# A fused attention and two-layer MLP kernel: the first batch's weight conversion one tile earlier, eight sums later, three attention steps in the next half

## The chip, the core and the metric

The kernel runs on one NeuronCore of a Trainium2 chip. The core has five engines that run side by side, each with its own queue of instructions in order: TensorE (PE, matmuls; its weight loads are PEld), VectorE (DVE), ScalarE (ACT), GpSimd (POOL) and SyncE (SP, which here only issues DMAs). The metric is the time of one execution on the device in microseconds (us), the median of several runs.

## The reference

Inputs are q, k, v of 4 batches, 8 heads, 768 positions and 64 channels a head, and an MLP's U, V, w_ch1 (512 x 2048) and w_ch2 (2048 x 512), the latter in float64.

```python
# attention: a band of +-15 keys, and one summary key for each block of 32
k_sum = k.reshape(B, H, nb, 32, D).max(axis=3)
v_sum = v.reshape(B, H, nb, 32, D).mean(axis=3)
scores_l = where(|i - j| < 16, scale * q @ k.T, -1e9)
scores_s = scale * q @ k_sum.T + log(32)
a = softmax(concat([scores_l, scores_s]))
x = a @ concat([v, v_sum])                 # heads side by side: 768 x 512 a batch
# the MLP
u = x + (x.T @ U @ V).T
out = u + relu(u @ w_ch1) @ w_ch2
```

## The kernel before

The four batches go through the MLP one after the other, and the attention of batch b+1 is done in pieces while batch b's MLP keeps TensorE busy. For each batch the MLP has an up half (u @ w_ch1, then `relu`) and a down half (times w_ch2). This document is about batch 0. Its up half is 16 tiles of 128 hidden channels, each tile four slots of 6 matmuls (`up`, L970; both halves of the tokens, two slots each), so 64 slots. Its down half is 96 slots, 16 tiles of 6: four slots with 3 matmuls of 512 columns, then two with 6 matmuls of 256 columns (`down_phase`, L1256). Every product is made of three matmuls on a high and a low part of each operand.

**The weights of batch 0** come as float64 words, 32 tiles (16 up, 16 down), and each passes through a fixed chain that `first_weights` spreads over the slots of the tile that is being multiplied, tile s. SP loads the words of tile s+7 (L778). ACT scales the words (`scale_weight`, L148). DVE makes a float32 of them in two steps (`from_f64`, L160 and L161). Then `split_weight` makes the two parts: ACT writes the high part (L176) and POOL subtracts it for the low part (L177). Only then can TensorE use the tile. In the kernel before, during tile s, the tile s+1 is split, s+2 is converted and s+3 is scaled. The first two or three tiles are done in `START`, an order written out by hand for the first stage: `Z` is a scaling, `Y m.0` and `Y m.1` the two conversion steps, `W` a split, `G` and `Go` make the operand u, `U` are the up half's first slots. DVE also adds and subtracts weights for later batches (`sum_weights`, L821 to L825), and SP stores converted weights and sums (L830 to L840).

**keep_rows** (L986) has POOL add the two parts of u to get u back, eight additions of 128 x 384, for the end of the batch where u is added to the result.

**Attention of batch 1** is a list of 32 steps (`later_steps`), spread evenly over slots: the first 13 (`FIRST_STEPS_1`) over slots 8 to 61 of the up half, the other 19 over slots 0 to 65 of the down half. Of head h: SP loads k and q (L198, L207), PE makes scores (L351, 24 matmuls), DVE and ACT the exponentials (L376, L386), DVE turns 32 x 32 squares (L406), SP writes them to DRAM (L411) and fetches them back in another order (`fetch_squares`, L419, four DMAs into the tile `at`, which has one buffer), and PE multiplies them with the values (`square_values`, L484, called the product of head h below). The fetch for head h+1 is issued in the step that holds the product of head h, since it writes the buffer which that product reads. The block sums of v go to POOL in pieces, one a slot (`add_vsum`, L255 to L269), and POOL spreads the block maxima of k (L328).

All engines take their instructions in the order in which the Python program emits them (a manual schedule); the tile library adds the waits.

Of the kernel before, what the change touches and what calls it, by code (L numbers as in the profile page):

```python
# [33 lines left out]
NF = DF // P  # L34
# [48 lines left out]
    K4 E12 V0 lq7 V5 V7 V3 lv2 lv3 lr Kp4 K7 Kp7 E13 S4 N1 E8 T10 V6 E9 lw0 S7 T11 N2 E14 T12 lw1  # L83
    T13 Q1 Q0 E15 N0 Qo1 Qo0 M1 Mo1 C11 N3 Bp5 I0 Bd6 T8 lw2 Dd5 Z0 Io0 C10 Dp4 T15 lw3 Y0.0 T9
    Y0.1 Bp4 Dp7 J0 C8 T14 V10 V11 Jo0 G0.0 G0.1 C9 Dp6 lw4 Z1 C14 V9 C13 Bp7 C12 W0 Y1.0 Y1.1 N5
    V8 V12 C15 N4 V13 V15 V14 N6 G1.0 lw5 N7 Go0.0 Go0.1 I2 Io2 U0.0.0 G1.1 Go1.0 Go1.1 lw6 J2 Jo2
    U0.1.0 G0.2 G0.3 Go0.2 Go0.3 G1.2 G1.3 Go1.2 Go1.3 U0.0.1 U0.1.1 W1 Z2
"""


# [5 lines left out]
def body(ctx: ExitStack, tc, q0, q1, k, v, vn, uv, w1, w2, mask, ident, rep, out):  # L96
# [23 lines left out]
    def weight_place(m, dt=F32):  # L120
        return wt.tile([P, 2 * DM], dt, name="place", tag=f"w{m % RING}")
# [22 lines left out]
    def scale_f64(words):  # L144


        hi = words.bitcast(F32).rearrange("p (n w) -> p n w", w=2)[:, :, 1]
        nc.scalar.activation(hi, hi, AF.Prelu, scale=BIAS, alpha=2.0**32)  # L148
# [22 lines left out]
    def run(steps, n=None):  # L171
        for _ in itertools.islice(steps, n):
            pass

    def split(hi, lo, val, engine):
        nc.scalar.copy(hi, val)  # L176
        engine.tensor_tensor(lo, val, f32(hi), ALU.subtract)  # L177
# [597 lines left out]
    def load_weight(m):  # L775

        words[m] = weight_place(m, I32)
        nc.sync.dma_start(out=words[m], in_=(w1, w2)[m // NF][:, m % NF].bitcast(I32))  # L778

    def scale_weight(m):  # L780
        scale_f64(words[m])

    def turn_weight(m):

        vals = yield from from_f64([words.pop(m)])
        w_kept[m] = vals[0]

    def by_parts(val):

        return val.rearrange("p (i k f) -> p k i f", k=2, f=P)  # L790

    def split_weight(m):
        t, val = weight_place(m, F32R), w_kept[m]
        if m < NF:
            t = t.rearrange("p (k s i f) -> p k s i f", k=2, s=2, f=P)
            val = by_parts(val)
            hi, lo = t[:, :, 0], t[:, :, 1]
        else:
            t = t.rearrange("p (s c) -> p s c", s=2)
            hi, lo = t[:, 0], t[:, 1]  # L800
        split(hi, lo, val, nc.gpsimd)
        w_split[m] = t
# [33 lines left out]
    def store_down(f):  # L836
        nc.sync.dma_start(out=down_there[f // 2, :, f % 2], in_=w_kept[NF + f])
# [179 lines left out]
    for _, t in vt0:  # L1017
        nc.gpsimd.memset(t[:NB], 0.0)

    turns = {m: turn_weight(m) for m in range(2)}  # L1020
    uv_val = []

    def turn_uv():
# [92 lines left out]
    turning = {}  # L1116

    def first_weights(s, q, n):


        f = s % NF

        def turn():
            if s + 2 < 2 * NF:
                if s + 2 not in turning:
                    turning[s + 2] = turn_weight(s + 2)
                run(turning[s + 2], 1 if q == 1 else None)

        if q == 0:
            if s + RING - 1 < 2 * NF:  # L1130
                load_weight(s + RING - 1)
            if 0 < s and s + 1 < 2 * NF:
                split_weight(s + 1)
            if s < NF and f % 2 == 0:
                sum_weights(f // 2, 0)
            if s >= NF:
                store_down(f)
        if q == 1:
            turn()
            if s < NF:  # L1140
                store_up(f)
        if q == 2:
            if s < NF and f % 2 == 0:
                sum_weights(f // 2, 1)
            turn()
            if s < NF and f % 2:
                store_sums(f // 2)
        if q == 3 and s + 3 < 2 * NF:
            scale_weight(s + 3)
        if q == n - 1:  # L1150
            w_kept.pop(s - 1, None)

# [297 lines left out]

    UP, DOWN = 7 * NF // 2 - 2, NF * NU
    FIRST_STEPS = 15
    FIRST_STEPS_1 = 13
    OPERANDS = ((45, 49, 55, 62, 67), (68, 73, 79, 88, 86))

    UP0 = 4 * NF - 2
# [2 lines left out]
    for b in range(B):  # L1459
        cur, ahead, after = ([*sts, None, None][b + i] for i in range(3))  # L1460
        todo = later_steps(ahead) if ahead else []
        n_first = FIRST_STEPS if b else FIRST_STEPS_1
        mine, theirs = todo[:n_first], todo[n_first:]
        up_last = UP if b else UP0
        steps = spread(mine, 4 if b else 8, up_last)
        if b == 0:
            phase = first_up_phase(cur, done)
            for n, j in enumerate((-4, -3, -2, -1)):
                steps.setdefault(n + 1, []).append((later_start, ahead, j))
            for n, (hf, c) in enumerate(itertools.product(range(2), range(NC))):  # L1470
                steps.setdefault(2 * n + 3, []).append((keep_rows, cur, hf, c))
        else:
            phase = up_phase(cur)
        if not ahead:
            sum_places(cur)
            for p in range(NF // 2 - 1):
                steps.setdefault(7 * p + 11, []).append((gate_sums, cur, p))
        last = []
        for i in itertools.count():
            try:  # L1480
                next(phase)
            except StopIteration as end:
                last = end.value or []
                break
            do(steps.get(i, ()))
            if b == 0:
                first_weights(i // 4, i % 4, 4)
            tick()
            drip()
            if i == up_last - 8 and ahead:  # L1490
                g = gate_high(cur, 0)
            if i == up_last - 6 and ahead:
                gate_low(*g)
            if i == UP - 4 and not ahead:
                phase7 = seven_phase(cur)
                next(phase7)
        if not ahead:
            for i, _ in enumerate(phase7):
                if i < 2:
                    do([last[i]])  # L1500
                if i == 3:
                    gate_sums(cur, NF // 2 - 1)
                tick()
            break
        steps = spread(theirs, 0, OPERANDS[0][-1] - 1)
        for u, x in operand_places(ahead):
            steps.setdefault(u, []).append(x)
        for i, x in enumerate(last):
            steps.setdefault(1 + 2 * i, []).insert(0, x)
        for i, _ in enumerate(down_phase(cur, g)):  # L1510
            do(steps.get(i, ()))
            if b == 0:
                first_weights(NF + i // NU, i % NU, NU)
                f, n = divmod(i, NU)
                if (f, n) in ((NF - 5, 4), (NF - 4, 1), (NF - 4, 4)):
                    fetch_weight()
                if (f, n) in ((NF - 3, 4), (NF - 2, 1), (NF - 2, 4), (NF - 1, 2)):
                    prepare()
            tick()
            drip()  # L1520
            if after and i % NU == 0:
                do([(later_start, after, j) for j in {7: (-6,), 9: (-5,), 11: (-4,), 13: (-3, -1), 14: (-2,)}.get(i // NU, ())])
# [93 lines left out]
```

## Time and profile before

| | us |
|---|---|
| median of 3 runs (637.68 to 639.45) | 639.23 |
| the profiled execution | 633.91 |
| its span, from the first to the last instruction | 632.1 |
| batch 0: first stage, to the first up matmul | 0 to 45.9 |
| batch 0: up half | 45.9 to 133.0 |
| batch 0: down half | 133.0 to about 220 |
| batches 1 to 3 | to 632.1 |

The profile is of one execution; its records begin and end about 1.8 us inside the measured time. A row of the timeline gives an instruction's start, its length and, in brackets, how long its engine sat idle before it and what ended that wait.

### The profile page before, as it was taken

What the parts mean: (1) busy time and instruction counts of PE and PEld (TensorE: products, weight loads), DVE (VectorE), ACT (ScalarE), POOL (GpSimd) and SP (SyncE); (2) the same over time, 40 slices, a digit from 0 to 9 for tenths busy, and PEclk for the clock granted to TensorE, in tenths of its full rate; (3) what the DMA queues carried; (4) which work ended last, traced back from release to release, by engine and by line L of the source; (5) the groups of instructions that cost most, each with busy time, mean ns of one, the idle gap of its engine ahead of it and who ended that gap; (6) DMA issues with size and microseconds to landing.
All of it is one profiled execution on the core that took longest, in us unless ns stands there. A gap on an engine that the chain in (4) does not pass through costs nothing.

```text
span 632.1 us, 14968 instructions
## 1 busy us (share of the span) xinstructions
PE 606.3 (96%) x5560; PEld 551.8 (87%) x5560; DVE 415.9 (66%) x1102; ACT 366.3 (58%) x810; POOL 324.8 (51%) x408
## 2 busy tenths in 40 slices
PE   4987899999999999999999999999999999999997
PEld 3776799988878899998888899998888899999997
DVE  4874947867766945567557974567546664449992
ACT  3754456666746567765634646675544447669550
POOL 2435956734237885788466976684231356630000
PEclk9999899999999999999999999999999999999999
DMA  9888679999895577987987686889997564365551
GB/s 223 226 305 249 210 215 308 323 304 305 255 284 145 172 226 216 268 245 235 294 237 229 189 274 198 262 256 270 283 280 233 154 225 135 118 216 175 160 192 50
DMA packets 91624, 144.51 MB, mean 229 GB/s; under 512 B 8864, under 2 KB 61472, under 8 KB 91552
## 3 DMA queue, kind: packets, MB, share of 16 engines
q1 hardware_dynamic: 91552, 143.56, 74.5%
q8 instruction: 44, 0.72, 0.5%
q14 instruction: 28, 0.23, 0.1%
HBM read 102.63 MB, written 40.89 MB: 227 GB/s over the span
## 4 chain that ended last, share of the span: by engine, by line
PE 80%; POOL 5%; issue 4%; DMA 4%; DVE 2%; ACT 2%; SPq 1%; POOLq 0%; ACTq 0%; DVEq 0%
PE acc L1256 27%; PE ps_h L1158 27%; PE acc L1368 9%; PE ps_h L970 8%; PE ps_s L351 3%; PE ps_x L484 3%; POOL place L177 2%; POOL place L255 1%; DMA place<-in_vn 1%; DMA at<-there 1%; DMA place<-in_q 1%; DMA whole<-up 1%; POOL x L986 1%; PE ps_m L615 1%; PE ps_t L454 1%
## 5 line engine op out<-in xcount | busy, mean ns | idle before, releaser
L912 POOL TENSOR_TENSOR parts<-whole,parts 128x512 fp32r<-128x512 f32 (+1 forms) x128 | 157.3, 1237 | 131.1 <-ACT parts L916 110.9
L1158 PE MATMUL ps_h<-op,parts 128*128 128x384 f32 x1008 | 180.1, 336 | 0.3 <-ACT place L1204 0.3
L1158 PEld LDWEIGHTS ps_h<-op,parts 128*128 128x128 f32 x1008 | 174.3, 188 | 3.0 <-issue 1.3
L1256 PE MATMUL acc<-gh,parts 128*128 128x256 f32 (+1 forms) x512 | 135.4, 343 | 0.0
L1256 PEld LDWEIGHTS acc<-gh,parts 128*128 128x128 f32 x512 | 88.5, 190 | 12.9 <-issue 1.7
L916 ACT CAST parts<-whole 128x512 fp32r<-128x512 f32 (+1 forms) x144 | 83.2, 584 | 10.0 <-DMA whole<-up 3.7
L1256 PE MATMUL acc<-gl,parts 128*128 128x512 f32 (+1 forms) x256 | 86.7, 339 | 0.0
L386 ACT ACTIVATE e<-e,neg 128x120 f32<-128x120 f32 x144 | 46.5, 386 | 62.5 <-DVE neg L376 62.5
L177 POOL TENSOR_TENSOR place<-val,place 128x512 fp32r<-128x512 f32 x32 | 45.2, 1413 | 72.5 <-ACT place L176 49.6
L970 PE MATMUL ps_h<-place 128*128 128x384 f32 x384 | 73.0, 346 | 6.7 <-POOL place L177 4.8
L970 PEld LDWEIGHTS ps_h<-place 128*128 128x128 f32 x384 | 67.5, 192 | 10.9 <-POOL place L177 6.8
L1231 DVE SCALAR_TENSOR_TENSOR gl<-place,gh 128x768 fp32r<-128x768 f32 x48 | 50.2, 1046 | 35.2 <-ACT gh L1227 35.1
L1256 PE MATMUL acc<-gh,place 128*128 128x512 f32 (+1 forms) x256 | 67.2, 342 | 0.4 <-POOL e L372 0.2
L1227 ACT ACTIVATE gh<-place 128x768 fp32r<-128x768 f32 x48 | 40.5, 844 | 26.7 <-PE acc L1256 26.6
L1256 PEld LDWEIGHTS acc<-gl,parts 128*128 128x128 f32 x256 | 48.6, 190 | 3.9
L376 DVE CUSTOM_DVE_ANT_0 e<-ps_s,mask_sb 128x120 f32<-128x120 f32 x144 | 32.8, 277 | 27.4 <-PE ps_s L351 27.3
L1256 PEld LDWEIGHTS acc<-gh,place 128*128 128x128 f32 x256 | 44.2, 190 | 7.2 <-issue 0.9
L1368 PE MATMUL acc<-place,parts 128*128 128x384 f32 x246 | 43.6, 334 | 0.0
L1256 PE MATMUL acc<-gl,place 128*128 128x512 f32 (+1 forms) x128 | 43.4, 339 | 0.2 <-DVE gl L1231 0.2
L1368 PEld LDWEIGHTS acc<-place,parts 128*128 128x128 f32 x246 | 42.7, 188 | 0.0
L1218 DVE TENSOR_TENSOR place<-place,ps_h 128x384 f32<-128x384 f32 x24 | 13.3, 555 | 36.1 <-ACT place L1217 36.0
L1184 DVE TENSOR_TENSOR place<-place,ps_h 128x384 f32<-128x384 f32 x24 | 13.2, 551 | 30.0 <-PE ps_h L1158 30.0
(155 smaller groups left out, 948.3 us busy)
## 6 DMA issues: line engine op xcount, KB each, us to landing
place<-in_w SPq DMA_DIRECT2D x32, 512.0 KB, 5.4
whole<-up SPq DMA_DIRECT2D x24, 512.0 KB, 4.3
there<-squares SPq DMA_DIRECT2D x24, 384.0 KB, 4.7
at<-there SPq DMA_DIRECT2D x96, 96.0 KB, 4.7
whole<-up SPq DMA_DIRECT2D x24, 384.0 KB, 3.3
whole<-down SPq DMA_DIRECT2D x16, 512.0 KB, 5.0
vt<-in_v SPq DMA_DIRECT2D x48, 146.2 KB, 4.6
kt<-in_k SPq DMA_DIRECT2D x24, 288.0 KB, 5.4
```

What stands on the lines that cost most here:

```text
L177: engine.tensor_tensor(lo, val, f32(hi), ALU.subtract)
L351: nc.tensor.matmul(ps[a][c : c + 64, i * KC : (i + 1) * KC], qt[r : r + 64, q0 : q0 + 64], kt[r : r + 64, k0 : k0 + KC], start=True, stop= ...
L376: nc.vector.tensor_tensor_reduce(out=e[:, u, :], in0=ps[:, i * KC : (i + 1) * KC], in1=mask_sb[:, m, :], scale=-SCALE, scalar=BIG, op0=ALU ...
L386: nc.scalar.activation(e[:, u, :], e[:, u, :], AF.Exp, bias=st.neg[h][:, u : u + 1], scale=-1.0,)
L912: engine.tensor_tensor(lo, whole, f32(hi), ALU.subtract)
L916: nc.scalar.copy(hi, whole)
L970: nc.tensor.matmul(ps[:, :NH], w_split[f][:, c % 2, part_w, c // 2], ut[:, c, :], start=(c == 0 and j == 0), stop=(c == NC - 1 and j == 2),)
L1158: nc.tensor.matmul(ps, a[:, sa, i], b[:, sb, i], start=(first and n == 0), stop=(n == 5), skip_group_check=not first,)
L1227: nc.scalar.activation(gh, h, AF.Relu)
L1231: nc.vector.scalar_tensor_tensor(gl, h, 0.0, f32(gh), ALU.max, ALU.subtract)
L1256: nc.tensor.matmul(place, w[:, part_w, c * P : (c + 1) * P], gt[:, q0:q1], start=(f == 0 and i == 0 and j == 0), stop=(f == NF - 1 and j = ...
L1368: nc.tensor.matmul(ps, w[:, part_w, off : off + P], g[part_g], start=((name, i) not in begun and j == 0), stop=(p == NF // 2 - 1 and j == ...
```

## The change

Four things change, all in batch 0. The split runs two tiles ahead instead of one, the conversion three instead of two and the scaling four instead of three; START is extended so that the first tiles fit this. The eight `keep_rows` move from every second slot from slot 3 (to 17) to every fourth slot from 28 (to 56). And 10 instead of 13 attention steps are in the up half, so steps 10 to 12 go to the down half, whose 22 steps then stand three slots apart (19 steps stood three or four apart).

```diff
-    V8 V12 C15 N4 V13 V15 V14 N6 G1.0 lw5 N7 Go0.0 Go0.1 I2 Io2 U0.0.0 G1.1 Go1.0 Go1.1 lw6 J2 Jo2
-    U0.1.0 G0.2 G0.3 Go0.2 Go0.3 G1.2 G1.3 Go1.2 Go1.3 U0.0.1 U0.1.1 W1 Z2
+    V8 V12 C15 N4 V13 V15 V14 N6 W1 G1.0 lw5 N7 Go0.0 Go0.1 I2 Io2 U0.0.0 G1.1 Go1.0 Go1.1 lw6 Z2 J2
+    Jo2 U0.1.0 G0.2 G0.3 Go0.2 Y2.0 Go0.3 G1.2 G1.3 Go1.2 Go1.3 U0.0.1 U0.1.1 Y2.1 Z3
...
-    turns = {m: turn_weight(m) for m in range(2)}
+    turns = {m: turn_weight(m) for m in range(3)}
...
-            if s + 2 < 2 * NF:
-                if s + 2 not in turning:
-                    turning[s + 2] = turn_weight(s + 2)
-                run(turning[s + 2], 1 if q == 1 else None)
+            if s + 3 < 2 * NF:
+                if s + 3 not in turning:
+                    turning[s + 3] = turn_weight(s + 3)
+                run(turning[s + 3], 1 if q == 1 else None)
...
-            if 0 < s and s + 1 < 2 * NF:
-                split_weight(s + 1)
+            if s + 2 < 2 * NF:
+                split_weight(s + 2)
...
-        if q == 3 and s + 3 < 2 * NF:
-            scale_weight(s + 3)
+        if q == 3 and s + 4 < 2 * NF:
+            scale_weight(s + 4)
...
-    FIRST_STEPS_1 = 13
+    FIRST_STEPS_1 = 10
...
-                steps.setdefault(2 * n + 3, []).append((keep_rows, cur, hf, c))
+                steps.setdefault(4 * n + 28, []).append((keep_rows, cur, hf, c))
```

On POOL, in the first tiles of the up half of the kernel before, the splits (L177) stand between pieces of v's sums (L255 to L266), the spreading of k's maxima (L328) and the sums of u (L986):

```order
L177 TENSOR_TENSOR place<-val,place 128x2x256
L255 TENSOR_TENSOR place<-place 128x256
L986 TENSOR_TENSOR x<-place 128x3x128
L255 TENSOR_TENSOR place<-place 128x128
L264 TENSOR_TENSOR place<-place 128x64
L986 TENSOR_TENSOR x<-place 128x3x128
L266 TENSOR_TENSOR vsum<-vsum,place 128x64
L328 COPY kt<-km 64x4x12 x4
L177 TENSOR_TENSOR place<-val,place 128x2x256
```

The same stretch of POOL in the changed kernel:

```order
L177 TENSOR_TENSOR place<-val,place 128x2x256
L255 TENSOR_TENSOR place<-place 128x256
L328 COPY kt<-km 64x4x12 x4
L255 TENSOR_TENSOR place<-place 128x128
L264 TENSOR_TENSOR place<-place 128x64
L266 TENSOR_TENSOR vsum<-vsum,place 128x64
L177 TENSOR_TENSOR place<-val,place 128x2x256
L269 TENSOR_SCALAR vsum<-vsum 128x64
```

The two sums of u that stood in each tile there are gone from it, and each split is of one tile later in the list of weights.

On SP, at the passage from the up to the down half of the kernel before, the fetch for the product of head 2 (the first L419 here) is followed by the up half's last weights, and the next fetch belongs to the down half:

```order
L419 DMA at<-there 32x4x192 x4
L221 DMA vt<-in_v 96x390
L222 DMA vt<-in_v 96x390
L830 DMA up_105<-val 128x512
L778 DMA place<-in_w 128x1024
L832 DMA up_105<-val 128x2x128
L840 DMA up_105<-place 128x1024
L778 DMA place<-in_w 128x1024
L837 DMA down<-val 128x512
L198 DMA kt<-in_k 128x3x192
L207 DMA qz_84<-in_q 64x384 x2
L419 DMA at<-there 32x4x192 x4
```

In the changed kernel the fetch for the product of head 2 stands in the down half, six slots ahead of that product, and the next fetch follows it:

```order
L837 DMA down<-val 128x512
L198 DMA kt<-in_k 128x3x192
L207 DMA qz_85<-in_q 64x384 x2
L411 DMA there<-squares 128x768
L419 DMA at<-there 32x4x192 x4
L221 DMA vt<-in_v 96x390
L222 DMA vt<-in_v 96x390
L778 DMA place<-in_w 128x1024
L837 DMA down<-val 128x512
L198 DMA kt<-in_k 128x3x192
L207 DMA qz_84<-in_q 64x384 x2
L419 DMA at<-there 32x4x192 x4
```

What moved is the fetch for the product of head 2, from the up to the down half, and with it the loads and stores of three steps.

## Rows read from the trace of the kernel before

**Rows 1.** The profile page, part 1: TensorE's busy time and share.

```profile
PE 606.3 (96%) x5560; PEld 551.8 (87%) x5560; DVE 415.9 (66%) x1102; ACT 366.3 (58%) x810; POOL 324.8 (51%) x408
```

**Rows 2.** Timeline of PE: up matmuls that waited (start, length, idle before, releaser).

```profile
54.67 0.62 PE L970 MATMUL ps_h<-place 128*128 128x384 f32 x2 [1.09 <-ACT place L176]
56.03 4.43 PE L970 MATMUL ps_h<-place 128*128 128x384 f32 x24 [0.74 <-POOL place L177]
61.82 0.96 PE L970 MATMUL ps_h<-place 128*128 128x384 f32 x4 [1.36 <-POOL place L177]
72.05 0.62 PE L970 MATMUL ps_h<-place 128*128 128x384 f32 x2 [0.79 <-ACT place L176]
74.92 6.98 PE L970 MATMUL ps_h<-place 128*128 128x384 f32 x28 [2.25 <-POOL place L177]
...
91.01 5.13 PE L970 MATMUL ps_h<-place 128*128 128x384 f32 x28 [0.47 <-POOL place L177]
```

**Rows 3.** Stretches: length, busy PE PEld DVE ACT POOL (count), granted clock, DMA share, GB/s.

```profile
66.00:75.00 9.00, 5.96 (x33) 5.12 (x31) 8.86 (x17) 4.35 (x10) 8.72 (x13) 1.00 0.74 214
75.00:83.00 8.00, 8.00 (x54) 7.28 (x55) 3.77 (x8) 1.53 (x3) 7.23 (x10) 0.79 0.47 139
97.00:133.00 36.00, 36.00 (x330) 34.68 (x331) 29.66 (x83) 22.62 (x50) 24.63 (x39) 1.00 0.99 307
133.00:160.00 27.00, 26.80 (x353) 21.54 (x352) 19.21 (x55) 18.02 (x38) 9.45 (x16) 1.00 0.97 298
```

**Rows 4.** Timeline of POOL, two sums of u and a split in tile 4.

```profile
67.95 1.18 POOL L986 TENSOR_TENSOR x<-place 128x384 f32<-128x384 f32 x1
...
70.43 1.01 POOL L986 TENSOR_TENSOR x<-place 128x384 f32<-128x384 f32 x1
...
73.49 1.38 POOL L177 TENSOR_TENSOR place<-val,place 128x512 fp32r<-128x512 f32 x1
```

**Rows 5.** Chain of waits: start, length and count of up matmuls in two stretches.

```profile
74.92 6.02 PE ps_h L970 x24
...
96.92 13.82 PE ps_h L970 x78
```

**Rows 6.** Line L986 (`keep_rows`): shortest, median and longest ns, first and last start.

```profile
L986 POOL TENSOR_TENSOR x<-place x8: 999/1097/1452, 57.7 to 81.4; 128x384 f32<-128x384 f32 x8
```

**Rows 7.** Timeline of DVE: conversion steps, and one subtraction alone and beside POOL.

```profile
52.95 0.42 DVE L822 TENSOR_TENSOR place<-place,val 128x256 f32<-128x256 f32 x1
53.29 0.42 DVE L160 TENSOR_SCALAR val<-place 128x512 int32<-128x512 int32 x1
...
73.78 1.37 DVE L822 TENSOR_TENSOR place<-place,val 128x256 f32<-128x256 f32 x1
...
83.87 0.69 DVE L161 SCALAR_TENSOR_TENSOR val<-place,val 128x512 int32<-128x512 int32 x1
```

**Rows 8.** Chain of waits: a head's scores, and six slots of the down half.

```profile
149.26 0.78 PE ps_s L351 x24
...
350.29 4.21 PE acc L1256 x24
```

**Rows 9.** Timeline of PE: products of heads 1, 3, 6 and 7.

```profile
125.09 0.89 PE L484 MATMUL ps_x<-vt,at 120*32 120x65 f32 x48
...
145.36 0.89 PE L484 MATMUL ps_x<-vt,at 120*32 120x65 f32 x48
...
174.74 0.89 PE L484 MATMUL ps_x<-vt,at 120*32 120x65 f32 x48
...
185.16 0.89 PE L484 MATMUL ps_x<-vt,at 120*32 120x65 f32 x48 [1.33 <-DMA at<-there]
```

**Rows 10.** Timeline of SP: issue of the fetches behind those of heads 1, 3, 6.

```profile
126.42 2.00 SPq L419 DMA_DIRECT2D at<-there  x4
...
147.10 3.73 SPq L419 DMA_DIRECT2D at<-there  x4
...
177.28 3.79 SPq L419 DMA_DIRECT2D at<-there  x4
```

**Rows 11.** DMA issues: a fetch's four transfers, KB each, median us to landing.

```profile
at<-there SPq DMA_DIRECT2D x96, 96.0 KB, 4.7
```

**Rows 12.** Line L778, loads of weights: us to landing, shortest, median, longest.

```profile
DMA to landing us min/median/max: 3.8/5.4/9.9
```

## The prediction

> **What bounds the kernel now.** I read part 1 of the page first: TensorE is busy for 606.3 us, 96% of the span [rows 1]. So a change helps only where it takes idle time or a slow clock from TensorE, and hurts only where it adds them. Next the timeline of PE alone over batch 0, looking for brackets. The up half has six matmuls that waited, 1.09, 0.74, 1.36, 0.79, 2.25 and 0.47 us, 6.70 us together, and each was released by one of the two instructions that split a weight tile, ACT's L176 or POOL's L177 [rows 2]. They lie between 54 and 91 us; from 97 to 133 us PE is busy for 36.00 of 36 us [rows 3].
>
> Why the splits were late is read from the stretches: from 66 to 75 us POOL is busy 8.72 of 9 us and DVE 8.86, while PE does 5.96 [rows 3]. The timeline of POOL shows what stands ahead of the split at 73.49, for which PE waited 2.25 us: among others two sums of u of 1.18 and 1.01 us [rows 4].
>
> The waits have a second price. In the stretch from 75 to 83 us the mean granted clock is 0.79, so for a part of it PE ran at the lower of its two levels (1.2 instead of 2.4 GHz), right behind the waits of 0.79 and 2.25 us [rows 2, 3]. The chain of waits gives the cost: 24 up matmuls took 6.02 us there, against 13.82 us for 78, 0.177 each, later [rows 5]. 24 x 0.177 = 4.25, so the slow clock cost 1.77 us. The waits of 1.09 and 0.74 us, two matmuls apart, and the one of 1.36 us were followed by no such row.
>
> **The change part by part.**
>
> Split one tile earlier. It removes no instruction. A tile of the up half is 24 matmuls, 24 x 0.177 = 4.25 us, and this is what each split gains in time before it is needed; the largest wait was 2.25 us, or 3.0 us with the 0.79 before it. ACT's cast still stands behind the copies of the tile before, which wait for PE, but then has a whole tile in hand. The sums of u leave the full stretch: eight at a median of 1.10 us [rows 6], 8.8 us of POOL, of which one and a half to two stood ahead of each split between 57 and 82 us. Either of the two edits would take most of the waits; with both I see none of the six left. Gain: 6.70 + 1.77 = 8.47 us.
>
> The scaling of a tile now comes 3.75 tiles behind its load instead of 4.75, 16 us; the longest landing of a weight load is 9.9 us [rows 12]. That costs nothing while the loads keep within this. The cover is thinner than it looks, since the DMA engines are busy at a share of 0.99 from 97 to 133 us [rows 3], but PE did not wait there.
>
> START. The scaling and conversion of tile 2 move ahead of the last operands u: DVE's two steps (0.42 and 0.69 us [rows 7]) stand among and behind the last four subtractions which the up matmuls wait for. Cost between 0 (PE busy with the transposes) and 1.1 us (both in the way). Only the first of the two stands ahead of a subtraction, so I take 0.4.
>
> The sums of u at slots 28 to 56. POOL has 24.63 us of work in the 36 us from 97 to 133 us [rows 3]; with eight sums it would have 33.4, still within the 36, and the three attention steps that leave give some back. Cost 0, hidden under a split that is two tiles ahead; without that cover, up to the 2.25 us of a wait.
> A row speaks against the place, though: DVE's 128 x 256 subtraction took 0.42 us while POOL rested and 1.37 us beside a POOL split [rows 7]. If each sum stretched DVE by its own length, 8.8 us more would stand on 29.66 of 36 us [rows 3], 2.4 us too much. The Trainium skill (GPSIMD Engine Reference, Key points) has the rule: GpSimd shares its SBUF interfaces with VectorE and contends with its instructions that read two SBUF inputs. The trace agrees on this pair. By the rule the up half would lose 2.4 us again, by the rows of rows 3 alone nothing; I take nothing, since a lag of 2.4 us is less than the 4.25 us gained.
>
> Three attention steps from the up to the down half. The steps 10 to 12 hold one head's scores, 0.78 us [rows 8], and one product, 0.89 us with its tail [rows 9]; that is as much less in the up half as more in the down half, so 0. Their ACT, DVE and SP work moves too, from a half with DVE at 82% to one with 71% (19.21 of 27 us [rows 3]). What is not neutral is the distance between the products in the down half. A fetch cannot start before the product of the head before it has read the buffer, and the next product waits for it. How long that loop takes, from the end of a product to the landing of the last of the four transfers, I work out from the issue rows plus 4.7 us of landing [rows 11], counted from the last issue's start (0.4 us before the group's end). Head 1: from 125.98 to 128.42 - 0.4 + 4.7, 6.7 us. Head 3: 146.25 to 155.1, 8.8 us. Head 6: 175.63 to 185.16, where PE really stood, 9.5 us [rows 9, 10]. The steps are now three slots apart. Between the products of heads 1 and 2 stand two steps, six slots, so PE has 4.21 + 0.78 = 5.0 us of work [rows 8]. Between the others stand nine slots, 1.5 x 4.21 = 6.3 us, plus 0.78 where a head's scores lie between (heads 2 to 3, 3 to 4, 4 to 5), 7.1 us. With the loop of each place, the new waits are: head 2, 6.7 - 5.0 = 1.7 us; head 3, none (6.7 against 7.1); head 4, 8.8 - 7.1 = 1.7 us; heads 5 and 6, none to 0.4; head 7, up to 9.5 - 6.3 = 3.2 us, of which I take half, 1.6, because batch 2's loads that sat ahead of this fetch on SP are now three slots further ahead of it. Sum 5.0 us, less the 1.33 us that PE waits for head 7 already: 3.7 us. The bounds: with the shortest loop everywhere (6.7) 1.7 + 2 x 0.4 - 1.3 = 1.2; with the longest everywhere (9.5) 4.5 + 3 x 2.4 + 2 x 3.2 - 1.3 = 16.8.
>
> **Sum.** -8.5 + 0.4 + 3.7 = -4.4 us. Made against the profiled execution of 633.91 us this is 629.5. That execution lies 5.3 us under the median of the runs, 639.23; I carry the difference over: 639.2 - 4.4 = 634.8 us.
>
> **The rivals.**
>
> The fetch loop takes the gain back (slower). If the loop takes the 9.5 us of head 6 at all six products, the down half gains 16.8 us of waits and the sum is -8.1 + 16.8 = +8.7, 647.9 us. It decides from a mean loop c with (c - 5.0) + 3(c - 7.1) + 2(c - 6.3) - 1.3 = 8.1, which is c = 8.1 us. For it: the DMA engines are at 0.97 in the first 27 us of the down half [rows 3], and three steps' transfers are added. Against it: two of the worked-out loops lie above 8.1 and one below [rows 9, 10], but both long ones had a group of loads issuing at that moment, and a PE that waits lets the queue run empty.
>
> The clock falls in the down half. After a wait of 2.25 us close behind another the clock fell and 1.77 us were lost [rows 2, 5]; the wait for head 2 may be that long. Two such falls: 634.8 + 3.5 = 638.3 us. The rows speak both ways, as 1.36 us alone did nothing. The Trainium skill (TensorE: Matmul & The Clock Gate, HAM oscillation) says that an array that waits for DMA again and again falls back to the half clock each time; no row of the down half shows it so far.
>
> The up half keeps half its waits, because POOL and DVE fall behind where the sums now stand, so the change does not do what it says: 4.2 us of the 8.5 are not gained, 639.0 us. For it: DVE's stretch beside POOL [rows 7]. Against it: PE's full 36 us from 97 to 133 us with less lead than it will have.
>
> The fetch loop is short everywhere: 632.3 us. For it: the loop of head 1 [rows 9, 10].
>
> **How the numbers follow.** A measurement of this kernel can tell about 0.3%, 1.9 us, from no change. Chances: forecast 0.54 (632.5 to 637.3), short loop 0.16, clock 0.12, up waits kept 0.09, long loop 0.09. The first two are faster and so is a little of the clock's case: 0.72. Same: 0.18, from the clock and the kept waits. Slower: 0.10. The range runs from 631 to 639.5 and leaves out the long loop and the tails.
>
> **What would show it.** Right: in the trace of the changed kernel no up matmul released by L176 or L177 after 54 us, a granted clock of 1.00 throughout, an up half shorter by about 10 us (8 of waits and clock, 1.6 moved), and a wait of 1 to 3 us ahead of the product of head 2, released by the fetch. Wrong: up matmuls that still wait for L177, or brackets ahead of every product whose sum is over 9 us, or a down half below 1.00 of the clock.

## The result and the profile after

The changed kernel takes 632.99 us (median of 10 runs, 629.48 to 635.63), the kernel before 638.61 in the same series (10 runs, 636.23 to 641.87). The ratio is 0.9907, with a 95% interval from 0.9878 to 0.9935: 5.6 us faster, where 4.4 were forecast.

The profiled execution of after took 632.76 us, with a span of 631.0. That is only 1.1 us under the 632.1 of before, because what lies outside the change differs from one execution to the next: the first stage lasted 45.9 us in before's profile and 48.2 in after's, and everything behind batch 0 lasted 412.1 and 413.3. A second profile of each kernel (the last two experiments) had 47.1 and 45.8 us for the first stage. So I compare the two halves of batch 0, each cut at its first matmul, to 0.2 us. The first fence is before, the second after; columns as in [rows 3], the up half first.

```profile
45.90:132.92 87.02, 80.28 (x624) 74.80 (x623) 60.46 (x155) 47.34 (x105) 56.78 (x87) 0.98 0.86 265
132.92:220.03 87.11, 84.75 (x839) 71.47 (x838) 64.11 (x129) 55.15 (x110) 43.22 (x48) 1.00 0.78 238
```

```profile
48.20:124.44 76.24, 75.28 (x552) 72.70 (x551) 63.13 (x138) 45.35 (x98) 51.15 (x69) 1.00 0.91 283
124.44:217.70 93.26, 88.47 (x910) 74.04 (x909) 66.10 (x147) 56.80 (x116) 51.05 (x66) 0.98 0.78 240
```

The first number behind the stretch is its length, the second how long PE was busy; the difference is PE's idle time. The up half became 10.8 us shorter: idle 6.74 us before, 0.96 after, and 5.0 us less busy time. The down half became 6.15 us longer: 3.7 us more busy, 2.4 more idle. The net is -4.6 us; between the second profiles it is -5.9.

What PE still waited for is in the timeline of PE of after, to be held against [rows 2] and the last line of [rows 9]:

```profile
61.98 1.38 PE L351 MATMUL ps_s<-kt,qz 64*64 64x120 f32 x24 [0.80 <-POOL kt L328]
63.29 16.94 PE L970 MATMUL ps_h<-place 128*128 128x384 f32 x96
...
131.51 0.84 PE L351 MATMUL ps_s<-kt,qz 64*64 64x120 f32 x22 [0.85 <-DVE x L498]
...
148.98 0.84 PE L351 MATMUL ps_s<-kt,qz 64*64 64x120 f32 x22 [0.49 <-DVE x L498]
...
183.71 1.53 PE L484 MATMUL ps_x<-vt,at 120*32 120x65 f32 x48 [3.16 <-DMA at<-there]
```

No up matmul waits for L176 or L177 any more; from 63 us 96 of them run in one piece of 16.94 us. In their place stand a wait of one head's scores for the block maxima of k, two waits of scores for DVE's normalise step (L498), and 3.16 us for the fetch of head 7. The stretches of [rows 3] now read:

```profile
66.00:75.00 9.00, 9.00 (x54) 9.00 (x53) 8.86 (x19) 5.09 (x11) 8.48 (x15) 1.00 0.72 214
75.00:83.00 8.00, 8.00 (x67) 7.59 (x66) 5.21 (x14) 4.77 (x11) 4.36 (x6) 1.00 0.97 314
...
133.00:160.00 27.00, 26.32 (x353) 21.19 (x352) 23.06 (x65) 16.86 (x38) 14.56 (x26) 1.00 0.96 267
160.00:190.00 30.00, 26.74 (x291) 22.04 (x290) 19.35 (x44) 17.14 (x33) 6.97 (x5) 0.94 0.90 280
```

From 66 to 75 us POOL and DVE are as full as before (8.48 and 8.86 of 9 us), but PE lives on its lead and does 9.00 us instead of 5.96. The clock of 0.79 from 75 to 83 us is gone. A new one is there, 0.94 from 160 to 190 us.

TensorE's busy share is as before [rows 1], in a shorter span (the page, part 1):

```profile
PE 605.6 (96%) x5560; PEld 552.1 (87%) x5560; DVE 419.7 (67%) x1102; ACT 366.2 (58%) x810; POOL 326.9 (52%) x408
```

### The profile page after: what moved, and what is told of

It reads as the page before. It is cut to its first block, busy times and chain, and to the rows that moved or that the text cites. A ratio compares the mean times of both kernels' runs of the same rounds, so it can differ in the third digit from the quotient of the medians.

```text
span 631.0 us, 14969 instructions
## 1 busy us (share of the span) xinstructions
PE 605.6 (96%) x5560; PEld 552.1 (87%) x5560; DVE 419.7 (67%) x1102; ACT 366.2 (58%) x810; POOL 326.9 (52%) x408
## 4 chain that ended last, share of the span: by engine, by line
PE 79%; DMA 5%; DVE 5%; issue 3%; ACT 3%; SPq 2%; POOL 1%; ACTq 0%; POOLq 0%; DVEq 0%
PE acc L1256 27%; PE ps_h L1158 26%; PE acc L1368 9%; PE ps_h L970 9%; PE ps_s L351 3%; PE ps_x L484 3%; DMA at<-there 2%; DMA whole<-up 1%; DMA place<-in_q 1%; DMA place<-in_vn 1%; DVE val L160 1%; DVE gl L1231 1%; DMA place<-in_k 1%; ACT e L386 1%; DVE val L161 1%
## 5 line engine op out<-in xcount | busy, mean ns | idle before, releaser
L1256 PEld LDWEIGHTS acc<-gh,parts 128*128 128x128 f32 x512 | 88.4, 189 | 12.9 <-issue 1.7
L177 POOL TENSOR_TENSOR place<-val,place 128x512 fp32r<-128x512 f32 x32 | 47.1, 1474 | 61.6 <-ACT place L176 45.4
L1256 PE MATMUL acc<-gh,place 128*128 128x512 f32 (+1 forms) x256 | 69.0, 346 | 0.0
L970 PE MATMUL ps_h<-place 128*128 128x384 f32 x384 | 68.9, 337 | 0.0
```

What stands on the lines that cost most here:

```text
L970: nc.tensor.matmul(ps[:, :NH], w_split[f][:, c % 2, part_w, c // 2], ut[:, c, :], start=(c == 0 and j == 0), stop=(c == NC - 1 and j == 2),)
L1256: nc.tensor.matmul(place, w[:, part_w, c * P : (c + 1) * P], gt[:, q0:q1], start=(f == 0 and i == 0 and j == 0), stop=(f == NF - 1 and j = ...
```

## The experiments

Each was timed against the kernel before in the same series (5 to 12 runs; the last two, one run). Intervals are 95%. Diffs are against the changed kernel unless said.

### The three steps go back

```diff
-    FIRST_STEPS_1 = 10
+    FIRST_STEPS_1 = 13
```

> The changed kernel with one part undone: 13 attention steps stay in the up half. Theory A (the longer lead and the late sums take the up half's waits, and the moved steps only cost): the up half has no wait on L176 or L177, it is about 78 us long (76.2 in the changed kernel plus 1.6 of moved TensorE work), and the down half falls from 93.3 us back to about 87, with no wait of over 1.5 us for the fetch of head 7. Time about 4.5 us under the changed kernel, some 10 us under the kernel before, ratio to before 0.984 to 0.988. Rival B (the fewer steps are what frees POOL and DVE in the up half): waits on L177 come back in the up half, 3 us or more in sum, and the ratio is 0.991 to 0.996.

Measured: 627.66 us, ratio 0.984 [0.982, 0.986], in its profile an up half of 77.8 us and a down half of 86.7. Against its own before it gains 9.7 us (637.38 - 627.66), the whole change 5.6: moving the steps costs 4.1 us. In the profile the steps take 1.6 us out of the up half and put 6.6 into the down half. The wait ahead of head 7's product was longer than expected:

```profile
178.22 0.89 PE L484 MATMUL ps_x<-vt,at 120*32 120x65 f32 x48 [1.87 <-DMA at<-there]
```

This kernel has the same 623 or 624 matmuls in its up half as before, so its busy time there prices the waits' side costs:

```profile
48.00:125.80 77.80, 76.83 (x623) 73.76 (x622) 65.64 (x149) 47.51 (x106) 56.34 (x82) 1.00 0.94 295
```

80.28 - 76.83 = 3.45 us of PE's busy time went with the waits (the two cuts may be off by 0.1 us), against 1.77 counted for the slow clock.

### The sums early again

```diff
-                steps.setdefault(4 * n + 28, []).append((keep_rows, cur, hf, c))
+                steps.setdefault(2 * n + 3, []).append((keep_rows, cur, hf, c))
```

> The changed kernel with one part undone: the eight sums of u stand early again, at slots 3 to 17. Theory A (the lead of one more tile, 4.25 us, covers the POOL backlog of the early tiles, whose largest wait was 3.0 us): the up half has at most 1 us of waits on L177 and the time is within 1.5 us of the changed kernel. Rival C (POOL is over its capacity in tiles 1 to 6, so any lead is used up and the sums had to go): waits on L177 of 3 us or more in tiles 3 to 6, and 3 to 5 us more than the changed kernel.

Measured: 640.45 us, 1.0036 [1.0015, 1.0057]. With the lead and the moved steps but without the late sums, the whole gain is gone, 7.5 us against the changed kernel and more than either theory gave. In the profile the up half has two waits on POOL. The timeline of PE and the stretch behind it:

```profile
63.52 1.38 PE L351 MATMUL ps_s<-kt,qz 64*64 64x120 f32 x24 [1.65 <-POOL kt L328]
...
85.33 1.05 PE L970 MATMUL ps_h<-place 128*128 128x384 f32 x4 [2.70 <-POOL place L177]
```

```profile
66.00:75.00 9.00, 9.00 (x45) 9.00 (x45) 8.83 (x19) 5.03 (x13) 8.84 (x13) 0.83 0.45 131
```

POOL is busy for 8.84 of 9 us, and its timeline shows the order in which the pieces stand; two sums of 1.2 to 1.5 us lie between two splits:

```profile
69.88 1.72 POOL L177 TENSOR_TENSOR place<-val,place 128x512 fp32r<-128x512 f32 x1
71.56 0.93 POOL L255 TENSOR_TENSOR place<-place 128x256 f32<-128x256 f32 x1
72.45 1.46 POOL L986 TENSOR_TENSOR x<-place 128x384 f32<-128x384 f32 x1
...
74.94 1.20 POOL L986 TENSOR_TENSOR x<-place 128x384 f32<-128x384 f32 x1
...
76.61 1.46 POOL L177 TENSOR_TENSOR place<-val,place 128x512 fp32r<-128x512 f32 x1
```

The two splits stand 6.7 us apart, where a tile lasts 4.25. A lead of one tile is used up in less than two such tiles. A lead delays the waits; it does not remove the overload.

### The lead undone

START, `turns` and the four offsets are those of the kernel before; the sums stay late, the steps moved.

```diff
-            if s + 2 < 2 * NF:
-                split_weight(s + 2)
+            if 0 < s and s + 1 < 2 * NF:
+                split_weight(s + 1)
...
-        if q == 3 and s + 4 < 2 * NF:
-            scale_weight(s + 4)
+        if q == 3 and s + 3 < 2 * NF:
+            scale_weight(s + 3)
```

> The changed kernel with one part undone: split, conversion and scaling with the kernel before's lead, the sums late and 10 steps in the up half. Theory A: the waits of tile 1 (1.09 and 0.74 us in the kernel before) stay, as POOL was idle ahead of them, and some of tile 2's 1.36; those of tiles 4 and 7 go, and the clock stays at 1.00. So some 2 to 3 us of waits in the up half, and the time 2 to 3 us over the changed kernel, ratio to before 0.994 to 0.997. Rival C (the sums were the whole cause): no waits in the up half, time as the changed kernel.

Measured: 641.07 us, 1.0054 [1.0032, 1.0077], worse than either theory gave it. The profiled execution, 636.27 us, was the shortest of its runs, so its rows show less than the usual cost. Part of the difference is the clock: the mean granted clock of a run was 1.00 in the profiled execution and 0.989 to 0.997 in the eleven others, median 0.993 over all. At half speed for a time t a run loses t/2, so a mean clock c costs about 1 - c of the span, by this estimate 0.007 x 639 = 4.5 us; where in the span those runs lost it is not on record. Even in the profiled execution:

```profile
113.53 4.44 PE L970 MATMUL ps_h<-place 128*128 128x384 f32 x24 [2.02 <-POOL place L177]
134.49 0.50 PE L1256 MATMUL acc<-gh,place 128*128 128x512 f32 x1 [0.68 <-POOL place L177]
```

Without the lead the late sums make a wait where there was none before: 2.02 us at 113 us, and splits for the down half come late too (0.68, 0.68 and 0.64 us).

### The loads of batch 2 later

The first group of loads for batch 2's attention (L247 and others, on SP) goes from slot 42 to slot 48 of the down half.

```diff
-                do([(later_start, after, j) for j in {7: (-6,), 9: (-5,), 11: (-4,), 13: (-3, -1), 14: (-2,)}.get(i // NU, ())])
+                do([(later_start, after, j) for j in {8: (-6,), 9: (-5,), 11: (-4,), 13: (-3, -1), 14: (-2,)}.get(i // NU, ())])
```

> The changed kernel, with batch 2's first loads (block sums of v, k and q of head 0) issued at slot 48 of the down half, behind the fetch for head 7, instead of at slot 42 ahead of it. Theory D (those loads, ahead of the fetch on SP and on the DMA engines, make the 3.16 us wait for head 7 and with it the fall of the clock): the wait is under 1 us, the granted clock stays at 1.00 from 184 to 188 us, and the time is 3 to 4.5 us under the changed kernel, ratio to before about 0.985. Rival E (the chain of DVE work of head 7, whose squares were turned at 169.5 us, sets the fetch): the wait stays at 2 us or more and the time moves by less than 1.5 us.

Measured: 628.14 us, 0.9851 [0.9827, 0.9875]. The wait for head 7 is gone and so is the slow clock behind it; the down half takes 88.4 us instead of 93.3. Why shows in SP's queue: first after, then this kernel.

```profile
170.47 0.34 SPq L411 DMA_DIRECT2D there<-squares  x1
...
172.84 0.90 SPq L247 DMA_DIRECT2D place<-in_vn  x2
173.78 1.23 SPq L198 DMA_DIRECT2D kt<-in_k  x1
175.06 1.38 SPq L207 DMA_DIRECT2D qz<-in_q  x2
176.54 2.40 SPq L419 DMA_DIRECT2D at<-there  x4
```

```profile
170.72 0.34 SPq L411 DMA_DIRECT2D there<-squares  x1
...
173.50 2.69 SPq L419 DMA_DIRECT2D at<-there  x4
...
177.66 0.90 SPq L247 DMA_DIRECT2D place<-in_vn  x2
```

In after, three groups of loads stand between the product of head 6 (ended 173.04) and the fetch for head 7. The fetch's first issue came 3.50 us after that product's end, and 0.20 us in this kernel (173.30 to 173.50); the time from the first issue to the last landing changed less, 7.0 and 6.5 us. So most of the wait is the order on SP's queue, and little the load on the DMA engines. The chain of waits of after runs through the loads, from DVE's squares over the store and the load to the fetch and the product:

```profile
169.47 0.98 DVE squares L406
170.47 0.34 SPq L411
...
172.84 5.77 DMA place<-in_vn
178.63 4.95 DMA at<-there
183.71 1.53 PE ps_x L484 x48
```

### Each edit alone

The lead alone has the diffs of the first two experiments together (13 steps, sums early).

> The kernel before with the longer lead alone (split two tiles ahead, conversion three, START extended); sums of u early, 13 attention steps in the up half. Theory F (lead and late sums are worth something only together: with the early sums POOL has more work in tiles 1 to 6 than it can do, so one tile of lead is eaten up by tile 6; without the lead each late split is seen at once): the up half keeps 4 us or more of waits on POOL and some slow clock, ratio to before 0.993 to 1.000. Rival G (the parts add up: lead and sums together gave 10 us with 13 steps, and each has about its half): ratio 0.990 to 0.994.

Measured: 633.67 us, 0.9942 [0.9917, 0.9967]. Its up half takes 82.0 us. The splits' waits are nearly gone (0.84 and 0.22 us), but a head's scores wait for k's maxima, which stand on POOL behind a sum of u, and the clock falls:

```profile
60.58 2.01 PE L351 MATMUL ps_s<-kt,qz 64*64 64x120 f32 x24 [1.67 <-POOL kt L328]
```

```profile
58.00:66.00 8.00, 6.21 (x45) 5.36 (x44) 3.83 (x11) 2.93 (x7) 7.65 (x14) 0.79 0.52 167
```

The late sums alone (13 steps, lead undone):

> The kernel before with the late sums alone (slots 28 to 56); lead and attention steps as before. Theory F: waits on L176 and L177 stay in tile 1 (1.8 us in sum, POOL idle ahead of them) and come up where the sums now stand, about tile 13 (2.0 us in the run without the lead and with 10 steps); up half 83 to 85 us; ratio to before 0.994 to 1.000. Rival G: the waits of tiles 4 and 7 go and nothing comes for them, ratio 0.990 to 0.994.

Measured: 636.82 us, 0.9989 [0.9967, 1.0011], no difference. In its profile (640.10 us, the longest of its twelve runs) the early waits shrink, from 6.7 to 3.9 us, and new ones come where the sums went, this one and 0.89 us at 124 us, so that the sum is 6.7 us as before:

```profile
107.53 2.58 PE L970 MATMUL ps_h<-place 128*128 128x384 f32 x10 [1.94 <-POOL place L177]
```

The ratio of the lead alone lies between the ranges of the two theories, and its waits on POOL, 2.7 us, are fewer than the 4 of theory F. What decides against rival G is the sum: 3.4 us for the lead and nothing measurable for the sums, against 9.7 us for both.

The moved steps alone, against the kernel before:

```diff
-    FIRST_STEPS_1 = 13
+    FIRST_STEPS_1 = 10
```

> The kernel before with the third part alone: 10 attention steps in the up half, 22 in the down half. Theory A (the moved steps only cost): the up half keeps its waits on L176 and L177, within 1 us of the 6.7 us of the kernel before, and the down half has a wait of 2.5 to 4 us for the fetch of head 7 and about 1.3 us at scores that wait for DVE (L498); 5 us more than the kernel before, ratio 1.005 to 1.010. Rival B (fewer steps relieve POOL and DVE in the early tiles, so the waits there shrink by 3 us or more): ratio 0.999 to 1.003.

Measured: 644.17 us, 1.0102 [1.0073, 1.013]. The up half is no shorter (87.4 us), because the waits for splits grow by what the steps free, from 6.7 to 8.8 us, more than either theory gave them. The down half takes 94.6 us; four splits come late there too (0.25, 0.68, 0.69 and 0.64 us), head 7 waits 1.68 us and the clock falls behind it. The longest wait of the up half:

```profile
82.73 6.72 PE L970 MATMUL ps_h<-place 128*128 128x384 f32 x28 [3.47 <-POOL place L177]
```

### The best of it

13 steps and the loads at slot 48, the diffs of the first and the fourth experiment together:

> Lead and late sums with 13 steps in the up half, and batch 2's first loads at slot 48 of the down half. With 13 steps the fetch for head 7 is issued at slot 45, still behind a load at 42 and now ahead of one at 48. Theory D: its wait of 1.87 us goes to under 0.5 us; ratio to the kernel before 0.980 to 0.982, 2 us under the kernel with 13 steps and early loads. Rival: with 13 steps the fetch had time enough but for the DMA engines' load, so the wait stays over 1 us and the time within 0.7 us.

Measured: 624.68 us, 0.980 [0.9773, 0.9827], faster than both kernels. Its five runs were granted a mean clock of 0.997 to 1.000, the 18 of the kernel before beside them 0.986 to 0.997 (median 0.993, 4.5 us by the working above), so about a third of the 12.4 us is clock. In the two halves PE is idle for 0.94 and 0.63 us:

```profile
46.00:124.00 78.00, 77.06 (x623) 73.98 (x624) 65.84 (x149) 47.86 (x106) 56.55 (x83) 1.00 0.93 297
124.00:209.00 85.00, 84.37 (x841) 71.79 (x840) 63.65 (x137) 54.06 (x109) 47.64 (x54) 1.00 0.79 247
```

To that, POOL's first spreading of k's maxima one slot group earlier, so that the scores need not wait 0.8 us:

```diff
-                steps.setdefault(n + 1, []).append((later_start, ahead, j))
+                steps.setdefault(1 if j == -1 else n + 1, []).append((later_start, ahead, j))
```

> As the one with 13 steps and late loads, and the spreading of k's maxima for head 0 emitted at slot 1 instead of slot 4, ahead of four pieces of v's sums on POOL. Theory: the 0.81 us for which the first scores wait for POOL (L328) is a matter of POOL's order alone and goes; 0.5 to 0.9 us less than the kernel without this edit, ratio to before 0.979 to 0.981. Rival: the wait moves to the next instruction (split of tile 3 behind it), no difference.

Measured: 624.33 us, 0.9802 [0.9775, 0.9829], the same. The 0.8 us went, but 0.46 us for L177 at 73 us, as the rival had it, and 0.68 us for a fetch at 146 us came.

### The late loads in the kernel before, and two second looks

The late loads alone (the fourth experiment's diff), put into the kernel before:

> The kernel before with batch 2's first loads at slot 48 of the down half instead of 42, nothing else. Theory D: its wait of 1.33 us for the fetch of head 7 goes, ratio 0.997 to 0.999 (1.3 us is 0.2%). With lead, late sums and 13 steps the same move gave 3 us; if it gives that here too, the wait of head 7 in most executions is longer than in the profiled one.

Measured: 634.71 us, 0.995 [0.9923, 0.9976]. In its profile head 7's product does not wait. The gain, 3.4 us, is more than the 1.33 us that PE waits there in [rows 9]. Is that wait longer in other executions? The kernel before, unchanged, in a second profile:

> The kernel before, once more, for a second profile. Loads issued later in batch 0 (the experiment before) gained 0.5%, 3.2 us, where the profiled wait ahead of head 7's product is 1.33 us. If that wait varies from execution to execution, this profile shows it at 1.8 to 2.8 us, as the kernels with the same steps did (1.87, 1.97, 2.74), perhaps with a granted clock of about 0.95 from 160 to 190 us. If it does not vary, it is 1.2 to 1.5 us again, and the gain has another cause. The six waits of up matmuls should be there either way, 6 to 7 us together, with a clock near 0.8 from 75 to 83 us.

```profile
76.18 6.98 PE L970 MATMUL ps_h<-place 128*128 128x384 f32 x28 [2.26 <-POOL place L177]
...
187.08 0.89 PE L484 MATMUL ps_x<-vt,at 120*32 120x65 f32 x48 [2.00 <-DMA at<-there]
```

The six waits repeat to within 0.02 us, the wait for head 7 does not: 2.00 us. That is within the interval of the gain (0.24% to 0.77%, 1.5 to 4.9 us), though short of its middle. The clock gives about the rest: the eight runs with late loads were granted 0.997 (median), the 13 of the kernel before beside them 0.994, and 0.003 x 636 is 1.9 us. That those falls stood behind this wait is not shown: in some of the kernels the clock fell there (the last section), in neither profile of the kernel before. The changed kernel, unchanged, in a second profile:

> The changed kernel, once more, for a second profile. If its waits follow from the order of its instructions: the two waits of score matmuls for the normalise step, 0.85 and 0.49 us, and the wait of scores for the k maxima, 0.8 us, again within 0.1 us, and ahead of head 7's product 2.5 to 3.5 us. If the wait for head 7 varies from execution to execution, it is outside of that, while the others repeat.

```profile
129.04 0.84 PE L351 MATMUL ps_s<-kt,qz 64*64 64x120 f32 x22 [0.85 <-DVE x L498]
146.54 0.84 PE L351 MATMUL ps_s<-kt,qz 64*64 64x120 f32 x22 [0.51 <-DVE x L498]
180.62 1.16 PE L484 MATMUL ps_x<-vt,at 120*32 120x65 f32 x48 [2.69 <-DMA at<-there]
```

With 0.79 us for k's maxima these are the same four waits, 2.69 instead of 3.16 us for head 7. Its halves take 76.2 and 92.7 us.

## Why the prediction was right, and where it was not

The forecast (634.8 us) and its sum (-4.4 us) lie near the result (632.99 and -5.6 us), and the two halves came out as foreseen, one shorter and one longer. Several terms inside did not. Of the signs that the prediction named, no up matmul waits for a split and the up half is shorter by about 10 us; but the wait ahead of head 2 did not come, and one sign of being wrong did, a down half below 1.00 of the clock.

**Up half, the six waits.** Right: none of the six is left. PE's idle time fell by 5.8 us instead of 6.7, since one wait of 0.80 us came in (scores behind POOL's L328), which no step named.

**Up half, what waits cost beside the idle time.** Mis-sized: counted 1.77 us of slow clock, measured 3.45 us of busy time (first experiment). The rest lies at the two ends of a wait. An up matmul lasts 0.335 us (the median) and in one piece they start 0.175 us apart ((16.94 - 0.335) / 95), each overlapping the next; the last one ahead of a wait overlaps none, which is 0.16 us. Behind a wait the start takes 0.1 us longer: the two matmuls between two waits took 0.62 us [rows 2], where 0.175 + 0.335 = 0.51. That is an estimated 0.27 us a wait, 1.6 us for six; with the 1.77 us this is about the 3.45 measured. Some tenths stay open, since the kernel compared has a wait of its own (0.81 us, scores).

**"Either of the two edits would take most of the waits."** The clearest error. For the sums it is wrong: alone they leave 6.7 us of waits and gain nothing that can be measured. For the lead it holds only to the letter: alone it leaves 1.06 us of the six waits, but a head's scores wait 1.67 us instead, the clock still falls, and 0.6% is gained. Both together gain 1.6% (627.66 us). I argued from the size of one wait against the lead of one tile; what counts is POOL's load over several tiles. With the sums in their old place and the steps moved, two splits stand 6.7 us apart where a tile lasts 4.25; with the sums late but no lead, a sum ahead of a split is a wait again. The price that the prediction gave for a missing cover, "up to the 2.25 us of a wait", was about right (2.02 and 1.94 us); that it would come in both cases was not seen.

**START.** Predicted 0.4 us, and not visible: up to 56 us PE is busy for 7.77 of the first 7.80 us of the up half. The first stage ended at 45.8 to 47.6 us in the six profiles with the old START and at 45.8 to 48.9 us in the eight with the new one, a scatter in which 0.4 us can't be told.

```profile
48.20:56.00 7.80, 7.77 (x50) 7.21 (x49) 4.97 (x11) 4.47 (x10) 0.00 (x0) 1.00 1.00 298
```

**The sums' new place.** Right in its cost of nothing, and the row that spoke against it came true: beside a sum of u a conversion step took 1.51 instead of 0.69 us [rows 7], at 84.58 us and twice more up to 103 us. From 97 to 124 us PE was nevertheless busy for 27.00 of 27 us; the lead covered the lag, as argued.

```profile
84.34 1.20 POOL L986 TENSOR_TENSOR x<-place 128x384 f32<-128x384 f32 x1
84.58 1.51 DVE L161 SCALAR_TENSOR_TENSOR val<-place,val 128x512 int32<-128x512 int32 x1
```

**The moved steps as work.** Right: about 1.6 us out of the one half and into the other (76.83 - 75.28 = 1.55 us of busy time; 0.78 + 0.89 = 1.67 counted).

**The fetch loop.** Right in size, wrong in place. Predicted were 1.7 us for head 2, 1.7 for head 4, 1.6 for head 7. Head 2 waited not at all and head 4 for 0.19 us, while head 7 took 3.16 (2.69 in the second profile), the end of its bound. For head 2 the loop was shorter than the 6.7 us counted: its fetch landed at 135.92, 5.6 us behind the product of head 1, and 0.85 us of that passed in another wait (below). Head 4's loop took 8.4 us, near the 8.8 counted, but PE had 7.9 us of work and 0.49 of another wait in that time, not 7.1 us: nine slots hold 33 or 39 matmuls, here 39, and 36 were counted. The 8.8 itself was not what the kernel before did: there that fetch landed at 153.97, 7.7 us behind the product of head 3, so the median landing overstated it. Ahead of head 7 PE had 7.5 us of work instead of 6.3, since parts of batch 1's operands (L649, L657) stand there, so the wait is the loop's doing. The step that failed is the reason for halving it: that batch 2's loads would be further ahead of the fetch. They issued right ahead of it, since SP first had to wait for the store of squares, which DVE began to turn at 169.47 us; the loop took 10.7 us (173.04 to 183.71), more than the longest of the three that I had worked out. The fourth experiment shows it: with the loads behind the fetch the wait is gone.

**A wait that was not foreseen.** 0.85 and 0.49 us of scores for L498. In the program all PSUM tiles come from eight banks; the down half holds six for its sums, so that a product and the scores right behind it share two, and the second bank of the scores is the one that L498 still reads. That is read from the program, and no run changed it; the 0.85 us stands in all six profiles with 10 steps in the up half and in none of the eight with 13.

**The rivals.** The clock did fall in the down half, as that rival said, but once and not twice, behind the wait for head 7: the four microseconds after it, in after's profile, were granted 0.61.

```profile
180.00:184.00 4.00, 0.84 (x15) 0.43 (x17) 2.23 (x5) 0.79 (x2) 0.29 (x1) 0.96 1.06 282
184.00:188.00 4.00, 4.00 (x61) 3.76 (x54) 0.92 (x3) 0.25 (x1) 0.00 (x0) 0.61 1.07 375
```

From 160 to 190 us the clock was 0.94: 0.06 x 30 / 0.5 = 3.6 us at the lower level, 1.8 us lost. The down half's bill is then 1.55 of moved work, 1.34 for L498, 1.83 more for head 7, 1.8 of clock: 6.5 us, against 6.15 measured. The rival of the long loop failed: two of the six loops in after were over its 8.1 us, head 4's (8.4) and head 7's (10.5 to the landing), the others 4.5 to 6.4, and the mean is 6.9. The rival of the kept waits failed, as none of the six is left. The rival of the short loop, 632.3 us, lies nearer to the time measured than the forecast does (as a difference, -6.9 against -5.6 measured, it is no nearer than -4.4). Its mechanism is right for four of the six, but it has no wait of 3.16 us and no slow clock in it, so that its number came close is luck.

So the size of the total was right partly because errors offset each other: the up half gave 1.1 us more than counted (10.8 instead of 9.7), the down half cost about 0.9 us more than counted (6.15 instead of 5.3), and the runs' medians differ by 1 us more than the first pair of profiles. The third edit is a loss wherever it was tried (4 us beside the other two, 6 us alone), and the change is faster in spite of it.

Why the moved steps alone cost 6 us and beside the lead and the late sums 4 shows, at least in direction, in the profiles: without the lead, POOL still sets the pace of the up half, whose waits for splits grow by 2.1 us, so the 1.6 us of moved work are not gained there, and four late splits cost 2.3 us in the down half, where the changed kernel has none. Two buffers for `at`, which might end the loop of fetch and product, were not tried.

## What to carry to other kernels

Waits that come from an overfull engine need both a lead, to bridge the overload, and less work in it, to let the lead last; price such edits together and apart, and compare an engine's work between two needed results with the time in which they are used up. Work moved to a place with room on every engine can still wait there for a buffer with one copy, for a PSUM bank, or behind loads in the issuing queue: look at what stands on that queue in the same microseconds. And cut a stage at its first matmul and read busy and idle time apart, since a wait also costs some tenths of a microsecond at its ends and sometimes the clock. A profile is one execution: its time and clock against those of the other runs tell how far it speaks for them.

## What the runs showed of the hardware

The length of a single wait does not tell whether the clock falls. Ahead of the same product, head 7's, waits of 1.68 and 1.97 us (the moved steps alone, the late sums alone) were followed by four microseconds at 0.58 and 0.67, and waits of 1.77, 1.87 and 2.00 us (the lead undone, the steps back, the second profile of before) by 1.00. In the up half it fell behind 1.65 and 1.67 us (the sums early, the lead alone) and stayed behind 2.02 and 2.12 (the lead undone, the moved steps alone). The two rows are of the moved steps alone and of the steps back, behind the wait of 1.68 and of 1.87 us:

```profile
196.00:200.00 4.00, 4.00 (x37) 3.02 (x36) 1.76 (x4) 0.84 (x1) 0.00 (x0) 0.58 1.07 374
```

```profile
182.00:186.00 4.00, 4.00 (x41) 3.18 (x41) 2.21 (x4) 1.62 (x3) 0.83 (x1) 1.00 0.92 284
```

The Trainium skill (TensorE: Matmul & The Clock Gate, HAM oscillation) tells of a kernel that waits for a DMA in every tile and falls back to the half clock each time. These runs agree for all six waits of 2.69 us and more in the two halves, two of them for POOL (2.69, 2.70, 2.74, 3.16, 3.47 and 4.00 us), and show both outcomes below.

POOL's splits can also stretch a conversion step with a single tile as input: DVE's L160, 0.42 us in [rows 7], took 1.56 us in after beside the split that began at 140.63, and 1.50 to 1.54 us in five other places there. In all six the split had begun first; the two L160 that began 0.04 and 0.02 us ahead of a split (at 69.96 and 111.05) took 0.41 and 0.38 us.

```profile
140.89 1.56 DVE L160 TENSOR_SCALAR val<-place 128x512 int32<-128x512 int32 x1
```
